# Gated linear attention and a routed mixture of experts: key transposes folded into the score products, single-pass running counts, and a planner that counts instruction pages

## The chip, the cores and the metric

One core of one Trainium2 chip runs the whole program. The metric is the device time of one execution in microseconds; three runs of the kernel before are known, with a median of 393.44 us. One more execution was taken with the hardware profiler, and every row below comes from that one.

## The reference, cut to what matters

The first half is a gated linear attention. For each of 4 batches and 8 heads, 768 steps in order:

```
state = alpha[t][:, None] * state + outer(k[t], v[t])      # 48 x 48 per head
y[t]  = q[t] @ state
```

The second half takes the 3,072 rows of y (384 wide, the heads side by side). For every token it computes logits against 8 experts and one local gate, picks an expert (the argmax, or the expert of the token before it where the gate is at least one half), and computes

```
out[t] = p[e] * (relu(x[t] @ w1[e]) @ w2[e])               # w1: 384 x 1024, w2: 1024 x 384
```

where p is the softmax probability of the chosen expert. Everything is float32.

## The kernel before, in words

**Blocks.** The attention runs in 24 blocks (`NB`) of 128 steps: block i is batch i mod 4 (`G` = 4), part i // 4 of the sequence. So blocks 0 to 3 start the four sequences, from an empty state, and blocks 20 to 23 end them. A block has two chunks c of 64 steps and four head pairs hp; the two heads of a pair, `par` 0 and 1, lie on partitions 64 to 111 and 0 to 47.

**A block's work.** `load` and `load_v` (lines 454 to 479) bring alpha (tile `xa`), keys and queries (`xkq`) and values (`vt`) through SP's queue. `mid` (485) has ACT put ones between the chunks. `scans` (489) has DVE run two reverse running products of alpha over it (`sf`), a reciprocal, and one forward running product (`A`); POOL then multiplies the keys by `sf` and the queries by `A`. `carry` (510) has POOL scale the state that the block takes over. On TensorE: `kt` (522), four transposes of the scaled keys, which ACT copies to the tile `kk`; `pm` (534), 16 score products k^T q, of which ACT copies one half and POOL masks it, while DVE masks the other half (tile `pq`); `um` (572), 8 products of `kk` with the values, which DVE adds to the state (`st`); `ym` (592), 16 products of `pq` with the values (`pv`) and 16 of the queries with the states (`ys`), into one pair of PSUM banks; then ACT copies the result to `XR`, SP stores it in DRAM, and `xt` (637) transposes it for the routing. A float32 product is two matmul instructions, each with a weight load: 16 products show as 32 matmuls.

**Routing.** After every fourth block `route` (662) computes logits, argmax, the gated choice, and each token's place in its expert's list. For the places it adds running counts (lines 731 to 737): the count so far, a triangle times the one-hot choices, and four products with a tile of ones, all float32.

**Experts.** The most popular expert's first 256 tokens are the job "0a" (gathered once 16 blocks are routed), the rest of it "0b", the other experts follow as r1 to r7. Weights and activations are split into a high and a low float32r part; each product is three matmuls. Gathers and stores by token run on POOL's queue.

**What sets the order.** The class `Plan` (76) holds every piece of work as a task: engine, estimated cost, priority, the names it reads and writes, the PSUM banks it needs. `order` (116) simulates the five queues with these costs and takes, on each engine, the open task of the lowest priority number; what it puts out is the program order of each engine, fixed before the run. Where TensorE would be idle for over 0.6 us, it puts products of a zero tile `dz` there ("fill"). `load_` (293) holds a load back until no more than 900 KB (`FLIGHT`) of earlier loads are under way. In `order` nothing stands for the fetching of TensorE's instructions from memory. Nearly all instructions are issued through one helper, so that their line in the profile is 269; they are told apart by the tiles.

Of the kernel before, what the change touches and what calls it, by code (L numbers as in the profile page):

```python
# [19 lines left out]
DM = H * D  # L20
# [4 lines left out]
C = 64  # L25
# [13 lines left out]
HALF = True  # L39
# [18 lines left out]
WS = 9  # L58
NX = dict(a=4, k=6, q=6)
# [11 lines left out]
class Task:  # L71
    __slots__ = ("eng", "cost", "fn", "prio", "deps", "succ", "left", "ready", "alloc", "free", "land", "port", "n", "end",
                 "moe", "start", "ap", "pre", "slack")


class Plan:
# [3 lines left out]
    FILL = 0.112  # L80

# [7 lines left out]
    def add(self, eng, cost, fn, prio, reads=(), writes=(), alloc=None, free=(), land=0.0, port=False, moe=False, after=None, slack=0.0, at=0.0):  # L89
# [3 lines left out]
        t.slack = self.slack + slack  # L93
        deps = set()
# [21 lines left out]
    def order(self, fill_until, fill_from):  # L116
# [6 lines left out]
        held, moe_held = {}, 0  # L123
# [7 lines left out]
        hold = []  # L131
# [19 lines left out]
        while done < len(self.tasks):  # L151
# [33 lines left out]
            if kind is not True:  # L185
                if e == "PE" and fill_from <= now[e] and at > now[e] and now[e] < fill_until(self):
                    n = int((at - now[e] - 0.35) / self.FILL) if at - now[e] > 0.6 else 0
                    b = [x for x, f in free.items() if f <= now[e]]
                    if n > 0 and b:
                        b = min(b, key=lambda x: free[x])  # L190
                        out.append((now[e], len(out), ("fill", b, n)))
                        filled += n * self.FILL
                now[e] = max(at, now[e] + 1e-6)
                continue
# [24 lines left out]
            end = at + t.cost  # L219
            now[e] = end  # L220
# [12 lines left out]
            for nm in t.free:  # L233
                got, m = held.pop(nm)
                for x in got:
                    free[x] = end + 0.06
                if m:
                    moe_held -= len(got)
# [18 lines left out]
def gla_moe(ctx, tc, akq, vw, vn, wg, w1, w2, cst, tok, out):  # L257
# [76 lines left out]
    one = cp.tile([128, 128], F32, name="one")  # L334
    trif = cp.tile([128, 128], F32, name="trif")
# [36 lines left out]
    Xs = dict(a=many(ap, NX["a"], [R, SW + 1], "xa"), kq=many(ap, NX["k"], [128, 2 * BW], "xkq"))  # L372
# [3 lines left out]
    KKs = many(ap, 2, [128, HP, R], "kk")  # L376
# [14 lines left out]
    def setup():  # L391
        add("DVE", 0.3, lambda: v_.memset(zz, 0.0), -9, writes=["zz"])
        add("DVE", 0.2, lambda: v_.tensor_copy(dz, zz[:, 0:256]), -9, reads=["zz"], writes=["dz"])
        add("DVE", 0.3, lambda: v_.memset(Zs, 0.0), -9, writes=["Z"])
        add("DVE", 0.1, lambda: v_.memset(P[0:R, 0, 129:HW:130], 1.0), -9, writes=["Z"])
        for j in range(NV):
            add("POOL", 0.4, lambda j=j: g_.memset(Vs[j][64:128, 0, :], 0.0), -5 + j, writes=[("vz", j)])
        for j in range(G):
            add("POOL", 0.25, lambda j=j: g_.memset(S3s[j][:, 0], 0.0), -4 + j, writes=[("S0", j)])
            add("POOL", 0.35, lambda j=j: g_.memset(S3s[j][96:128, 1:], 0.0), -3.9 + j, writes=[("S1", j), ("S2", j)])  # L400
        add("ACT", 0.4, lambda: s_.dma_start(cs, cst), -3.995, writes=["cs"], land=1.0)
        add("DVE", 0.1, lambda: v_.tensor_copy(DESC, cc("desc")), 2.0, reads=["cs"], writes=["desc"])
        add("ACT", 0.4, lambda: s_.dma_start(tk, tok), -2.5, writes=["tk"], land=0.5)
        add("ACT", 0.5, lambda: s_.dma_start(wgs, wg[:, :, 0:32]), -0.5, writes=["wgs"], land=0.5)
        add("ACT", 0.5, lambda: s_.dma_start(xd[0:1], zz[0:1, :]), 2, reads=["zz"], writes=["xd0"], land=0.1)
        add("POOL", 0.3, lambda: g_.memset(one, 1.0), 2.1, writes=["one"])
        for j in range(2):
            add("POOL", 0.15, lambda j=j: g_.memset(EXs[j][:, :, 8:], 1e-9), 2.2, writes=[("exx", j)])

        def f():  # L410
            g_.tensor_copy(PL[:, 1].rearrange("p (g b) -> p g b", b=G), tk[:, 0:2 * NB:2].rearrange("p (b g) -> p g b", b=G))
            g_.tensor_copy(PL[:, 2], tk[:, 1:2 * NB:2])
            g_.tensor_scalar(PL[:, 1], PL[:, 1], float(-SENT), None, ALU.add)
        add("POOL", 0.7, f, 2.55, reads=["tk"], writes=["plc"])
        kb0 = [e * RS - 1 + e / 16.0 - (16384.0 if e in EARLY else 0.0) for e in range(E)]
        for e in range(E):
            def consts(e=e):
                g_.memset(c0[:, e:e + 1], float(e * RS - 1))
# [3 lines left out]
            add("POOL", 0.4, consts, 2.3, writes=["cst"])  # L422
        add("POOL", 0.6, lambda: (g_.tensor_copy(trif, cc("tri")), g_.memset(trif[0:64, 64:128], 1.0),
                                  g_.memset(trif[64:128, 0:64], 0.0)), 2.4, reads=["cs"], writes=["trif"])
        add("POOL", 0.1, lambda: g_.memset(fill, 0.0), 2.9, writes=["fill"])
        add("PE", 0.3, lambda: t_.matmul(ps("io")[:, 0:128], lhsT=one, rhs=trif, start=True, stop=True), 2.6,
            reads=["one", "trif"], writes=["io"], alloc=("io", 1))
        add("DVE", 0.2, lambda: v_.tensor_scalar(io, ps("io")[:, 0:128], -1.0, None, ALU.add), 2.7, reads=["io"], writes=["iota"],
            free=["io"])

        def f():
            for x in range(NS):
                g_.tensor_scalar(ih[:, x], c0, float(1 + 128 * x), None, ALU.add)
        add("POOL", 0.7, f, 2.8, reads=["cst"], writes=["ih"])

    marks = {}
    OHs = many(rp_, 2, [128, E, G], "oh")
# [11 lines left out]
    def tile_of(c, i):  # L449
        if c == "a":  # L450
            return Xs[c][i % NX[c]]
        return Xs["kq"][i % NX[c]][:, 0:BW] if c == "k" else Xs["kq"][i % NX[c]][:, BW:]

    def load(c, i):
        at = i % G * NBB + i // G

        def go(o, r, w, cost, land, prio, reads, writes):
            add("SP", cost, lambda: load_(i, o, akq[r, at, w]), i - 4 + prio, reads=reads, writes=writes, land=land,
                at=FIRST * max(i - 1, 0) if i < NX[c] else 0.0)
        if c == "a":  # L460
            X, w = Xs["a"][i % NX["a"]], slice(2 * BW, 2 * BW + SW + 1)
            if i < NX["a"]:
                go(X[0:R], slice(0, R), w, 0.4, 0.85, 0, [], kx("a", i))
# [8 lines left out]
        else:  # L472
            for n, r in enumerate((slice(0, D), slice(C, C + D))):
                go(X[r], r, slice(0, 2 * BW), 0.36, 0.56, 0.01 + n * 0.002, [], [(x, i % NX["k"], n) for x in "kq"])

    def load_v(i):
        at, V = i % G * NBB + i // G, Vs[i % NV]
        add("SP", 0.4, lambda: load_(i, V[:, 1, :], vn[:, at * DM:(at + 1) * DM]), i - 1.9, writes=[("v1", i % NV)],
            land=0.55, at=FIRST * i if i < NV else 0.0)
# [42 lines left out]
    def kt(i):  # L522
        k, _ = kq(i)
        kk, nm = KKs[i % 2], f"kp{i}"

        def f():
            kp = ps(nm)[:, 0:HP * R].rearrange("p (h r) -> p h r", h=HP)
            for hp in range(HP):
                t_.transpose(kp[:, hp, :], k[0:R, hp, :], ident[0:R, 0:R])
        add("PE", 0.5, f, i, reads=kx("k", i) + ["cs"], writes=[nm], alloc=(nm, 1))  # L530
        add("ACT", 0.52, lambda: s_.copy(kk.rearrange("p h r -> p (h r)"), ps(nm)[:, 0:HP * R]), i + 0.02, reads=[nm],
            writes=[("kk", i % 2)], free=[nm])

    def pm(i):
        k, q = kq(i)
        pq, nm = PQs[i % 2], f"pe{i}"

        def f():
            pe = ps(nm, 2)
            for hp in range(HP):  # L540
                for (par, c) in ((0, 0), (1, 1), (0, 1), (1, 0)):
                    w = slice(c * C, (c + 1) * C)
                    r = slice(0, C) if par else slice(C, 128)
                    t_.matmul(pe[c * C:(c + 1) * C, par, hp * C:(hp + 1) * C], lhsT=k[r, hp, w], rhs=q[r, hp, w],
                              start=True, stop=True)

        def m():
            v_.tensor_tensor(pq, ps(nm, 2)[:, :, 0:HP * C].rearrange("p e (h t) -> p e h t", h=HP),
                             cc("tri")[:, 0:C].unsqueeze(1).unsqueeze(1).broadcast_to([128, 2, HP, C]), ALU.mult)
        add("PE", 0.65, f, i + 0.1, reads=kx("k", i) + kx("q", i), writes=[nm], alloc=(nm, 2))  # L550
# [4 lines left out]
        def pv(x):  # L555
            return ps(nm, 2)[:, x, 0:HP * C].rearrange("p (h t) -> p h t", h=HP)
        if i >= NB - 2 or MASK(i):
            marks[i] = add("DVE", 0.67, m, i + 0.15, reads=[nm, "cs"], writes=[("pq", i % 2, 0), ("pq", i % 2, 1)], free=[nm])
            return
        if HALF:  # L560
            add("ACT", 0.32, lambda: s_.copy(pq[:, 1], pv(1)), i + 0.14, reads=[nm], writes=[("pq", i % 2, 1)])
            add("POOL", 0.63, lambda: g_.tensor_tensor(pq[:, 1], pq[:, 1], tri(1), ALU.mult), i + 0.15, reads=["cs"],
                writes=[("pq", i % 2, 1)], port=True)
            marks[i] = add("DVE", 0.36, lambda: v_.tensor_tensor(pq[:, 0], pv(0), tri(1), ALU.mult), i + 0.15, reads=[nm, "cs"],
                           writes=[("pq", i % 2, 0)], free=[nm])
            return
        add("ACT", 0.58, lambda: s_.copy(pq, ps(nm, 2)[:, :, 0:HP * C].rearrange("p e (h t) -> p e h t", h=HP)), i + 0.14,
            reads=[nm], writes=[("pq", i % 2, 0), ("pq", i % 2, 1)], free=[nm])
        marks[i] = add("POOL", 1.2, lambda: g_.tensor_tensor(pq, pq, tri(2), ALU.mult), i + 0.15, reads=["cs"],
                       writes=[("pq", i % 2, 0), ("pq", i % 2, 1)], port=True)  # L570
# [823 lines left out]
```

## Time and profile before

| | us |
|---|---|
| median of three runs | 393.44 (391.44 to 393.61) |
| profiled execution, its own time | 390.28 |
| its span, first to last instruction | 388.4 |
| TensorE busy | 359.2 (92%) |
| VectorE (DVE) busy | 227.9 (59%) |
| ScalarE (ACT) busy | 183.0 (47%) |
| GpSimd (POOL) busy | 228.2 (59%) |

The time lies 1.9 us over the span. The span falls into a lead-in (0 to 10.7 us, no TensorE), the attention with its routing (to about 136 us, where the first expert product stands), and the experts. The shares of busy time are means over these; the attention is to be read by itself. A busy TensorE is not one at its peak: the ends of matmuls are modelled, and short products overlap.

### The profile page before, as it was taken

How to read it: one execution, taken by the hardware profiler on the slowest of the kernel's cores; microseconds unless marked ns; L12 is line 12 of the kernel's file. 1: busy time of each engine (PE TensorE's matmuls, PEld its weight loads, DVE VectorE, ACT ScalarE, POOL GpSimd, SP SyncE). 2: the span in 40 equal slices, each digit the busy share in tenths (PEclk: the TensorE clock that was granted, in tenths of full speed). 3: DMA queues.
4: the chain of work that ended last, by engine and by line, in shares of the span. 5: the costliest groups of instructions: out<-in, count | busy, mean ns of one | idle time of the engine just before them, and what ended most of it. 6: DMA issues, size and time to landing. Idle time of an engine off the chain costs nothing. (4 is left out here: it accounts for less than half of the span.)

```text
span 388.4 us, 11793 instructions
## 1 busy us (share of the span) xinstructions
PE 359.2 (92%) x4563; PEld 331.1 (85%) x4563; DVE 227.9 (59%) x545; ACT 183.0 (47%) x514; POOL 228.2 (59%) x329
## 2 busy tenths in 40 slices
PE   0897998988989899999999999999999999999993
PEld 0775787867878799998899999989999999999993
DVE  6796797889887877656434453542551552534320
ACT  2355755865675554374523552560561572542300
POOL 8897686889886523888782465456354354422002
PEclk9998999998999999999999999999999999999999
DMA  7899879869864261756744354553542542321001
GB/s 205 236 238 260 223 186 263 220 198 263 219 197 125 85 222 52 233 160 190 242 117 133 109 154 129 165 160 119 189 138 76 190 135 71 124 83 37 21 8 44
DMA packets 26156, 60.37 MB, mean 155 GB/s; under 512 B 4751, under 2 KB 11116, under 8 KB 26098
## 3 DMA queue, kind: packets, MB, share of 16 engines
q1 hardware_dynamic: 21888, 49.38, 44.0%
q0 software_dynamic: 3520, 9.91, 8.0%
q8 instruction: 37, 0.61, 0.7%
q10 hardware_dynamic: 690, 0.31, 0.3%
q14 instruction: 21, 0.17, 0.1%
HBM read 50.14 MB, written 9.91 MB: 155 GB/s over the span
## 5 line engine op out<-in xcount | busy, mean ns | idle before, releaser
L269 PE MATMUL P<-w2h,hb_mp 128*128 128x384 f32 (+3 forms) x432 | 116.3, 340 | 0.0
L269 POOL TENSOR_TENSOR w1l<-raw,w1h 128x256 fp32r<-128x256 f32 x96 | 70.0, 748 | 45.1 <-ACT w1h L269 33.3
L269 PEld LDWEIGHTS P<-w2h,hb_mp 128*128 128x128 f32 (+3 forms) x432 | 78.0, 185 | 2.0
L269 PE MATMUL P<-w2l,hb_mp 128*128 128x384 f32 (+4 forms) x232 | 78.3, 337 | 0.0
L269 DVE SCALAR_TENSOR_TENSOR hb_mp<-P,hb_mp 128x64 fp32r<-128x64 f32 (+6 forms) x104 | 41.3, 424 | 54.7 <-ACT hb_mp L269 54.3
L269 POOL DMA_INDIRECT out<-yo_mp,LI x27 | 27.4, 1014 | 72.8 <-DVE yo_mp L269 62.6
L269 ACT CAST w2h<-raw 128x384 fp32r<-128x384 f32 x64 | 32.2, 513 | 58.5 <-PE P L269 58.1
L269 PE MATMUL P<-xh_mp,w1h 128*128 128x448 f32 (+5 forms) x168 | 59.5, 354 | 0.0
L269 PE MATMUL P<-xh_mp,w1l 128*128 128x448 f32 (+5 forms) x168 | 59.3, 353 | 0.0
L269 PE MATMUL P<-xl_mp,w1h 128*128 128x448 f32 (+5 forms) x168 | 59.3, 353 | 0.0
L269 ACT ACTIVATE hb_mp<-P 128x448 fp32r<-128x448 f32 (+7 forms) x72 | 34.8, 484 | 52.0 <-PE P L269 47.2
L269 DVE TENSOR_SCALAR yo_mp<-P,LW 128x384 f32<-128x384 f32 (+3 forms) x23 | 14.0, 609 | 59.6 <-PE P L269 59.6
L269 PEld LDWEIGHTS P<-w2l,hb_mp 128*128 128x128 f32 (+4 forms) x232 | 41.4, 178 | 0.4
L269 ACT CAST w1h<-raw 128x256 fp32r<-128x256 f32 x96 | 36.7, 412 | 3.0 <-PE P L269 2.3
L269 DVE TENSOR_TENSOR w2l<-raw,w2h 128x384 fp32r<-128x384 f32 x64 | 35.8, 588 | 3.4 <-ACT w2h L269 3.3
L269 PEld LDWEIGHTS P<-xh_mp,w1l 128*128 128x128 f32 x168 | 31.5, 188 | 1.9
L269 PEld LDWEIGHTS P<-xl_mp,w1h 128*128 128x128 f32 x168 | 31.5, 188 | 1.9
L269 PEld LDWEIGHTS P<-xh_mp,w1h 128*128 128x128 f32 x168 | 31.5, 188 | 1.9
L269 DVE TENSOR_TENSOR_SCAN sf<-xa,P 112x260 f32<-112x260 f32 x48 | 31.3, 677 | 3.0 <-PE P L269 1.5
L269 POOL TENSOR_TENSOR xkq<-xkq,sf 112x512 f32<-112x512 f32 x24 | 28.4, 1182 | 7.2 <-DVE sf L269 5.3
L269 DVE TENSOR_TENSOR_SCAN A<-xa,P 112x520 f32<-112x520 f32 x24 | 29.6, 1233 | 4.0 <-PE P L269 2.2
L269 POOL TENSOR_TENSOR xkq<-xkq,A 112x512 f32<-112x512 f32 x24 | 28.4, 1183 | 3.7 <-DVE A L269 2.7
(159 smaller groups left out, 595.3 us busy)
## 6 DMA issues: line engine op xcount, KB each, us to landing
raw<-w SPq DMA_DIRECT2D x24, 512.0 KB, 3.8
raw<-w SPq DMA_DIRECT2D x32, 384.0 KB, 4.3
xkq<-akq SPq DMA_DIRECT2D x36, 192.0 KB, 4.6
vt<-vn SPq DMA_DIRECT2D x24, 192.0 KB, 4.1
xd<-XR SPq DMA_DIRECT2D x24, 192.0 KB, 4.5
xa<-akq SPq DMA_DIRECT2D x40, 97.7 KB, 4.2
xkq<-akq SPq DMA_DIRECT2D x12, 224.0 KB, 3.6
xa<-akq SPq DMA_DIRECT2D x4, 227.9 KB, 3.8
```

The lines of the kernel that those rows point to most:

```text
L269: r = f(*a, **k)
```

## The change

1. **Keys.** `kt` is gone. `pm` gives each of its 16 products a moving operand of 128 columns instead of 64: 64 columns of queries and a 64-column identity that is kept at the end of the tile `xkq`. The second half of each result is the transposed keys. ACT copies these to `kk` from the same PSUM banks, after its copy for `pq`.
2. **States.** In blocks 0 to 3, `ys` leaves out the products with the empty state of chunk 0, and the state is copied instead of added. In blocks 20 to 23, `um` computes only the first chunk's part (48 columns instead of 96).
3. **Running counts.** `one`, `trif` and the one-hot tile become float32r, with the layout block by expert; five of the six products become one matmul each.
4. **Planner.** It counts TensorE's instructions (`ins`), has a page of 256 of them, and stalls TensorE at a page's end until a fetch of 5.3, 4.6 or 3.6 us (by the time) that began when the page was entered is through. PSUM banks come free after the last task that uses them.
5. **Lead-in.** 28 zero products (`WARM`) run on TensorE ahead of the first block. The first activation-table load is forced early on ACT by an exponential of one element. Clears of tiles are spread over DVE, POOL and ACT; small constants leave POOL's early queue; the constants' load is cut in two and waits for the table; `mid` runs on DVE for blocks 0 and 1; the first loads come in another order, and those of the first two blocks are not held back by `FLIGHT`.

```diff
-HALF = True
+WARM = 28
+    PAGE, LEAD = 256, 63
+    def fetch(at):
+        return 5.3 if at < 45 else 4.6 if at < 110 else 3.6
...
+            if e == "PE":
+                c = count
+                count += t.ins
+                while count > edge:
+                    over = max(at, at + t.cost * (edge - c) / t.ins + end - at - t.cost)
+                    if over < there:
+                        self.stalled += there - over
+                        end += there - over
+                        over = there
+                    there = over + self.fetch(over)
+                    edge += self.PAGE
...
+        if n < 2:
+            return r
         flight.append((r.ins.name, o.shape[0] * o.free_size() * 4 / 1024))
...
-    one = cp.tile([128, 128], F32, name="one")
-    trif = cp.tile([128, 128], F32, name="trif")
+    one = cp.tile([128, 128], F32R, name="one")
+    trif = cp.tile([128, 128], F32R, name="trif")
-    Xs = dict(a=many(ap, NX["a"], [R, SW + 1], "xa"), kq=many(ap, NX["k"], [128, 2 * BW], "xkq"))
+    Xs = dict(a=many(ap, NX["a"], [R, SW + 1], "xa"), kq=many(ap, NX["k"], [128, 2 * BW + C], "xkq"))
-    KKs = many(ap, 2, [128, HP, R], "kk")
+    KKs = many(ap, 2, [128, 2, HP, C], "kk")
...
+        def warm():
+            for _ in range(WARM):
+                t_.matmul(ps("warm")[:, 0:240], lhsT=dz[:, 0:128], rhs=dz[:, 0:240], start=True, stop=True)
+        add("PE", WARM * 0.155, warm, -9, ins=2 * WARM, reads=["dz"], writes=["warm"], alloc=("warm", 1), free=["warm"])
-        add("ACT", 0.4, lambda: s_.dma_start(cs, cst), -3.995, writes=["cs"], land=1.0)
+        add("ACT", 0.4, lambda: s_.dma_start(cs[:, 0:256], cst[:, 0:256]), -8.9, reads=["table"], writes=["cs"], land=0.55)
+        add("ACT", 0.4, lambda: s_.dma_start(cs[:, 256:], cst[:, 256:]), -2.6, writes=["cs2"], land=0.45, at=6.0)
...
+        if i < 2:
+            add("DVE", 0.1, lambda: v_.memset(a[:, C + 1:SW:2 * (C + 1)], 1.0), i - 1.6, writes=kx("a", i))
+            return
...
-    def kt(i):
...
-                t_.transpose(kp[:, hp, :], k[0:R, hp, :], ident[0:R, 0:R])
-        add("PE", 0.5, f, i, reads=kx("k", i) + ["cs"], writes=[nm], alloc=(nm, 1))
-        add("ACT", 0.52, lambda: s_.copy(kk.rearrange("p h r -> p (h r)"), ps(nm)[:, 0:HP * R]), i + 0.02, reads=[nm],
-            writes=[("kk", i % 2)], free=[nm])
...
-                    t_.matmul(pe[c * C:(c + 1) * C, par, hp * C:(hp + 1) * C], lhsT=k[r, hp, w], rhs=q[r, hp, w],
-                              start=True, stop=True)
+                    x = X[r, at:at + C]
+                    t_.matmul(pe[c * C:(c + 1) * C, par, hp * 128:(hp + 1) * 128], lhsT=k[r, hp, c * C:(c + 1) * C],
+                              rhs=bass.AP(x.tensor, x.offset, [x.ap[0], (2 * BW - at, 2), (1, C)]), start=True, stop=True)
-        add("PE", 0.65, f, i + 0.1, reads=kx("k", i) + kx("q", i), writes=[nm], alloc=(nm, 2))
+        add("PE", 0.9, f, i + 0.1, ins=64, reads=kx("k", i) + kx("q", i) + [("xi", i % NX["k"])], writes=[nm], alloc=(nm, 2))
+        kc = lambda: add("ACT", 0.58, lambda: s_.copy(kk, part(1)), i + 0.145, reads=[nm], writes=[("kk", i % 2)], free=[nm])
...
+                    if i < G and not c:
+                        continue
...
-            t_.matmul(o, lhsT=ident, rhs=c_in.unsqueeze(2).broadcast_to([128, E, n + 1]), start=True, stop=False)
-            t_.matmul(o[:, :, 0:n], lhsT=trif, rhs=oh, start=False, stop=False)
+            t_.matmul(o, lhsT=ident, rhs=c_in.unsqueeze(1).broadcast_to([128, n + 1, E]), start=True, stop=False)
+            t_.matmul(o[:, 0:E * n], lhsT=trif, rhs=ot, start=False, stop=False)
             for x in range(1, n + 1):
-                t_.matmul(o[:, :, x:], lhsT=one, rhs=oh[:, :, 0:n + 1 - x], start=False, stop=(x == n))
+                t_.matmul(o[:, E * x:], lhsT=one, rhs=ot[:, 0:E * (n + 1 - x)], start=False, stop=(x == n))
...
+    add("ACT", 1.4, lambda: s_.activation(mark, one_r[0:1, 0:1], AF.Exp), -9, reads=["oner"], writes=["table"])
+    pads = ["DVE", "POOL", "ACT", "POOL", "ACT", "ACT"]
...
+    for j in range(NX["k"]):
+        for h in range(2):
+            r = slice(h * C, (h + 1) * C)
+            add("ACT", 0.2, lambda j=j, r=r: s_.copy(Xs["kq"][j][r, 2 * BW:], ident[r, r]), -6.5 + j, reads=["cs"],
+                writes=[("xi", j)])
...
-        kt(i)
```

## Rows read from the trace of the kernel before

**Rows 1.** Stretches: us; busy PE, PEld, DVE, ACT, POOL (instructions); clock, DMA, GB/s.
```profile
10.00:130.00 120.00, 106.92 (x2925) 90.66 (x2926) 99.61 (x234) 72.76 (x241) 97.74 (x143) 0.97 0.78 212
133.00:383.00 250.00, 249.27 (x1550) 237.61 (x1549) 119.65 (x287) 106.02 (x264) 119.88 (x144) 1.00 0.41 129
```
**Rows 2.** What TensorE waited for: us in total, times, longest.
```profile
PE P L269 <- POOL xkq L269: 10.7, 1, 10.7
PE P L269 <- issue: 7.6, 8, 2.2
```
**Rows 3.** TensorE in order of time, around 30 us: start, us, what.
```profile
28.50 0.80 PE L269 MATMUL P<-vt,pq 64*64 64x48 f32 x18
31.48 0.44 PE L269 MATMUL P<-vt,pq 64*64 64x48 f32 x14 [2.19 <-issue]
```
**Rows 4.** Stretches between such waits, the wait itself, and what follows it.
```profile
29.30:31.40 2.10, 0.00 (x0) 0.00 (x0) 1.96 (x5) 1.33 (x4) 2.04 (x3) 1.00 1.00 259
31.48:37.30 5.82, 5.16 (x127) 4.48 (x126) 2.80 (x7) 3.73 (x12) 3.65 (x5) 0.71 0.99 266
37.30:42.62 5.32, 4.48 (x127) 3.55 (x127) 4.40 (x8) 3.08 (x10) 5.32 (x7) 1.00 0.88 206
56.66:66.81 10.15, 8.72 (x253) 7.52 (x253) 8.33 (x20) 6.54 (x21) 7.50 (x10) 1.00 0.89 251
```
**Rows 5.** Instruction queue: packets, MB, share; whole span, 10 to 130 us, 136 to 384 us.
```profile
q8 instruction: 37, 0.61, 0.7%
...
q8 instruction: 23, 0.38, 1.5%
...
q8 instruction: 13, 0.21, 0.4%
```
**Rows 6.** The lead-in, in order of time; the median landing of the first alpha loads.
```profile
0.72 0.88 SPq L269 DMA_DIRECT2D xa<-akq  x2
5.70 1.28 ACT L269 ACT_TABLE_LOAD   x1 [5.70 <-DVE P L269]
7.22 1.28 DVE L269 TENSOR_TENSOR_SCAN sf<-xa,P 112x260 f32<-112x260 f32 x2 [1.45 <-ACT xa L269]
9.47 1.17 POOL L269 TENSOR_TENSOR xkq<-xkq,sf 112x512 f32<-112x512 f32 x1
...
xa<-akq SPq DMA_DIRECT2D x4, 227.9 KB, 3.8
```
**Rows 7.** TensorE in order of time: transposes and the next start; scores at 13.81 and 15.91.
```profile
18.77 0.60 PE L269 MATMUL P<-cs,xkq 112*128 112x112 f32 x4
19.21 0.49 PE L269 MATMUL P<-cs,XR 128*128 128x128 f32 x3
...
13.81 1.13 PE L269 MATMUL P<-xkq 64*64 64x64 f32 x32
...
15.91 0.69 PE L269 MATMUL P<-xkq 64*64 64x64 f32 x32
```
**Rows 8.** The same: products with states, with values, and a running count with its end.
```profile
17.35 0.68 PE L269 MATMUL P<-st,xkq 64*64 64x48 f32 x32 [0.29 <-ACT mark L269]
17.96 0.88 PE L269 MATMUL P<-vt,kk 128*48 128x96 f32 x16
...
130.56 0.39 PE L269 MATMUL P<-oh,trif 128*128 128x32 f32 x2
130.79 1.04 PE L269 MATMUL P<-oh,one 128*128 128x32 f32 x8
131.76 0.45 PE L269 MATMUL P<-st,xkq 64*64 64x48 f32 x16
```
**Rows 9.** ACT's two copies for a block, then all engines from 20 to 30 us.
```profile
15.03 0.37 ACT L269 COPY pq<-P 128x256 f32<-128x256 f32 x1 [2.66 <-PE P L269]
15.67 0.53 ACT L269 COPY kk<-P 128x448 f32<-128x448 f32 x1 [0.27 <-PE P L269]
...
20.00:30.00 10.00, 9.00 (x283) 7.34 (x275) 9.69 (x19) 4.51 (x15) 9.70 (x20) 1.00 0.94 246
```

More of the change, by code (lines that the diff above doesn't have):

```diff
@@ L87, in __init__, with add @@
         self.slack = 0.0
-    def add(self, eng, cost, fn, prio, reads=(), writes=(), alloc=None, free=(), land=0.0, port=False, moe=False, after=None, slack=0.0, at=0.0):
+    def add(self, eng, cost, fn, prio, reads=(), writes=(), alloc=None, free=(), land=0.0, port=False, moe=False, after=None, slack=0.0, at=0.0, ins=6):
         t = Task()
@@ L93, in add @@
         t.slack = self.slack + slack
+        t.ins = ins
+        t.uses = {k for k in (*reads, *writes) if isinstance(k, str)}
         deps = set()
@@ L130, in order @@
         filled = 0.0
-        hold = []
+        count, edge, there = self.LEAD, self.PAGE, 0.0
+        self.stalled = 0.0
+        users = {}
+        for t in self.tasks:
+            for k in t.uses:
+                users[k] = users.get(k, 0) + 1
         def fits(t, at):
@@ L232, in order @@
             t.end = fin
[L233 to L238, printed above, removed]
+            for nm in t.uses:
+                users[nm] -= 1
+                last[nm] = max(last.get(nm, 0.0), end)
+                if users[nm] == 0 and nm in held:
+                    got, m = held.pop(nm)
+                    for x in got:
+                        free[x] = last[nm] + 0.06
+                    if m:
+                        moe_held -= len(got)
             self.ap_left -= t.ap
@@ new lines, in warm @@
+        def warm():
+            for _ in range(WARM):
+                t_.matmul(ps("warm")[:, 0:240], lhsT=dz[:, 0:128], rhs=dz[:, 0:240], start=True, stop=True)
+        add("PE", WARM * 0.155, warm, -9, ins=2 * WARM, reads=["dz"], writes=["warm"], alloc=("warm", 1), free=["warm"])
+        for j in range(NV):
+            if j < 2:
+                add("POOL", 0.4, lambda j=j: g_.memset(Vs[j][64:128, 0, :], 0.0), -5 + j, writes=[("vz", j)])
+            else:
+                add("ACT", 0.5, lambda j=j: s_.copy(Vs[j][64:128, 0, :], zz[64:128, :]), -6 + j / 10, reads=["zz"],
+                    writes=[("vz", j)])
@@ L405, in setup @@
         add("ACT", 0.5, lambda: s_.dma_start(xd[0:1], zz[0:1, :]), 2, reads=["zz"], writes=["xd0"], land=0.1)
-        add("POOL", 0.3, lambda: g_.memset(one, 1.0), 2.1, writes=["one"])
+        add("DVE", 0.1, lambda: v_.tensor_copy(DESC, cc("desc")), 2.0, reads=["cs2"], writes=["desc"])
+        add("ACT", 0.25, lambda: s_.activation(one, zz[:, 0:128], AF.Copy, bias=1.0), 2.95, reads=["zz"], writes=["one"])
         for j in range(2):
-            add("POOL", 0.15, lambda j=j: g_.memset(EXs[j][:, :, 8:], 1e-9), 2.2, writes=[("exx", j)])
+            add("POOL", 0.15, lambda j=j: g_.memset(EXs[j][:, :, 8:], 1e-9), 3.0, writes=[("exx", j)])
@@ L415, in setup @@
+            s_.copy(PL[:, 2], tk[:, 1:2 * NB:2])
+        add("ACT", 0.4, f, 3.3, reads=["tk"], writes=["plc"])
         kb0 = [e * RS - 1 + e / 16.0 - (16384.0 if e in EARLY else 0.0) for e in range(E)]
@@ L421, in consts @@
                 g_.memset(lens[:, e:e + 1], float(LEN[e]))
[L422 to L426, printed above, removed]
+            add("POOL", 0.08, lambda e=e: g_.memset(c0[:, e:e + 1], float(e * RS - 1)), 3.2, writes=["cst0"])
+            add("POOL", 0.24, consts, 9.5 + e / 2, writes=["cst"], at=30.0 + 3 * e)
+        add("POOL", 0.6, lambda: (g_.tensor_copy(trif, cc("tri")), g_.tensor_copy(trif[0:64, 64:128], one.bitcast(F32)[0:64, 0:64]),
+                                  g_.tensor_copy(trif[64:128, 0:64], zz[64:128, 0:64])), 3.05, reads=["cs", "one", "zz"],
+            writes=["trif"])
+        add("POOL", 0.1, lambda: g_.memset(fill, 0.0), 4.9, writes=["fill"])
+        add("PE", 0.3, lambda: t_.matmul(ps("io")[:, 0:128], lhsT=one, rhs=trif, start=True, stop=True), 3.1, ins=4,
             reads=["one", "trif"], writes=["io"], alloc=("io", 1))
[L428 removed]
+        add("DVE", 0.2, lambda: v_.tensor_scalar(io, ps("io")[:, 0:128], -1.0, None, ALU.add), 3.2, reads=["io"], writes=["iota"],
             free=["io"])
@@ L458, in go @@
             add("SP", cost, lambda: load_(i, o, akq[r, at, w]), i - 4 + prio, reads=reads, writes=writes, land=land,
-                at=FIRST * max(i - 1, 0) if i < NX[c] else 0.0)
+                at=(0.0, 1.2)[i] if c == "a" and i < 2 else FIRST * max(i - 1, 0) if i < NX[c] else 0.0)
         if c == "a":
@@ L555, in pv @@
         def pv(x):
-            return ps(nm, 2)[:, x, 0:HP * C].rearrange("p (h t) -> p h t", h=HP)
+            return part(0)[:, x]
         if i >= NB - 2 or MASK(i):
-            marks[i] = add("DVE", 0.67, m, i + 0.15, reads=[nm, "cs"], writes=[("pq", i % 2, 0), ("pq", i % 2, 1)], free=[nm])
+            marks[i] = add("DVE", 0.67, m, i + 0.15, reads=[nm, "cs"], writes=[("pq", i % 2, 0), ("pq", i % 2, 1)])
+            kc()
             return
[L560 to L570, printed above, removed]
+        add("ACT", 0.32, lambda: s_.copy(pq[:, 1], pv(1)), i + 0.14, reads=[nm], writes=[("pq", i % 2, 1)])
+        add("POOL", 0.63, lambda: g_.tensor_tensor(pq[:, 1], pq[:, 1], tri(1), ALU.mult), i + 0.15, reads=["cs"],
+            writes=[("pq", i % 2, 1)], port=True)
+        marks[i] = add("DVE", 0.36, lambda: v_.tensor_tensor(pq[:, 0], pv(0), tri(1), ALU.mult), i + 0.15, reads=[nm, "cs"],
+                       writes=[("pq", i % 2, 0)])
+        kc()
     def um(i):
@@ L602, in pv @@
                     t_.matmul(yw[half(par, c), par, hp * D:(hp + 1) * D], lhsT=pq[r, par, hp, :], rhs=vt[r, h * D:(h + 1) * D],
-                              start=(hp == 0), stop=False, skip_group_check=True)
+                              start=(hp == 0), stop=(i < G and not c and hp == HP - 1), skip_group_check=True)
         def ys():
@@ L1130, in gla_moe @@
     one_r = ap.tile([R, HP], F32, name="one_r")
-    add("DVE", 0.1, lambda: v_.memset(one_r, 1.0), -9, writes=["oner"])
-    for n, (c, j) in enumerate((c, j) for j in range(max(NX.values())) for c in "kq" if j < NX[c]):
-        add("DVE" if n < 6 else "POOL", 0.55, lambda c=c, j=j, n=n: (v_ if n < 6 else g_).memset(tile_of(c, j)[96:128], 0.0),
-            -9.9 + n * 0.05 if n < 6 else -6.5 + n / 2, writes=[("xz", c, j)])
+    add("DVE", 0.1, lambda: v_.memset(one_r, 1.0), -9.95, writes=["oner"])
+    add("DVE", 0.36, lambda: v_.memset(zz, 0.0), -9.5, writes=["zz"])
+    add("DVE", 0.45, lambda: v_.tensor_copy(dz, zz[:, 0:256]), -8.95, reads=["zz"], writes=["dz"])
+    add("ACT", 1.4, lambda: s_.activation(mark, one_r[0:1, 0:1], AF.Exp), -9, reads=["oner"], writes=["table"])
+    pads = ["DVE", "POOL", "ACT", "POOL", "ACT", "ACT"]
+    for j in range(NX["k"]):
+        p = Xs["kq"][j][96:128, 0:2 * BW]
+        if pads[j] == "ACT":
+            add("ACT", 1.05, lambda p=p: s_.copy(p, zz[96:128, 0:1].broadcast_to([32, 2 * BW])), -8 + j, reads=["zz"],
+                writes=[("xz", c, j) for c in "kq"])
+        else:
+            for n, c in enumerate("kq"):
+                w = ("DVE", "POOL")[n] if j == 0 else pads[j]
+                e = dict(DVE=v_, POOL=g_)[w]
+                add(w, 0.53, lambda p=p, e=e, n=n: e.memset(p[:, n * BW:(n + 1) * BW], 0.0), -9.9 + j + n / 10,
+                    writes=[("xz", c, j)])
     for i in range(max(NX.values())):
@@ L1142, in gla_moe @@
             setup()
+    for j in range(NX["k"]):
+        for h in range(2):
+            r = slice(h * C, (h + 1) * C)
+            add("ACT", 0.2, lambda j=j, r=r: s_.copy(Xs["kq"][j][r, 2 * BW:], ident[r, r]), -6.5 + j, reads=["cs"],
+                writes=[("xi", j)])
     mp_box = []
```

109 lines of the change are left out of this document (52 added, 57 removed).

## The prediction

> **What bounds the kernel now.** First the busy times by stretch [rows 1]. From 133 us to the end TensorE works 249.27 of 250 us: the experts are TensorE's, the change touches nothing in them, and they start when the attention lets them. So the question is how much earlier TensorE gets through the attention. There, from 10 to 130 us, it is busy 106.9 of 120 us, DVE 99.6, POOL 97.7: three engines in fixed orders, none free by much, TensorE nearest to full.
>
> Second, TensorE's waits [rows 2]: 10.7 us for the first scaled keys, then mostly "issue", 7.6 us in 8 waits, up to 2.2 us, where no other engine is waited for. Third, such a wait in order of time [rows 3]: a run of 32 equal products breaks after 18 and goes on 2.19 us later, with no operand new. Fourth, the instructions between these waits [rows 4]: from 31.48 to 37.30 us 127 matmuls and 126 weight loads, then 127 and 127, then (two steps) 253 and 253. With a few semaphore waits each step is 256. Fifth, the instruction queue [rows 5]: 37 packets of 16 KB in the whole span, 23 of them in these 120 us, 13 in the 248 us of the experts. So TensorE's program arrives in pages of about 256 instructions, and in the attention, where 32 products take 0.69 us [rows 7], a page is used up about as fast as the next arrives: 120 / 23 = 5.2 us a page on average, and 5.32, 5.82 and 5.08 us in steps that ended in a wait [rows 4], with the data transfers busy 88 to 99%. During the wait itself they are at 100% [rows 4].
>
> **The change, part by part,** against the profiled execution's 390.28 us.
>
> *Lead-in.* DVE's first scan stands at 7.22 us, behind ACT's fill-in of ones, which stands behind a table load from 5.70 to 6.98 us [rows 6]. The first alpha tile is issued at 0.72 us and lands after about 3.8 us [rows 6], at 4.5. With DVE writing the ones itself (0.1 us by the planner's cost), the scan starts near 4.6: 2.6 us earlier. POOL's first multiply, at 9.47 us behind its clears, can follow the two scans at 4.6 + 1.28 = 5.9, or when the clears left to it are through (five pads, two value and four state clears, about 0.5 us each by the planner's costs: 0.7 + 5.5 = 6.2). That is 3.3 us earlier, and DVE's 2.6 decides. Both queues are full from 20 to 30 us, 9.7 of 10 [rows 9], so a shift of both is kept. **-2.6 us**; bounds 0 (alpha lands no sooner than ACT was ready, 7 us) and -4.5 (POOL's constants, which leave its queue too). The identity copies, the other pads and the table go to ACT, which first works at 5.70 us [rows 6]. The constants, now issued behind the table, about 0.9 + 1.3 us, land near 6 if they take 3.8 like the alpha tiles; the identity copies then have until the first scores at 6.2 + 2 x 1.17 = 8.5, so I cost them at 0. If the constants land later, the scores wait for them, and the gain goes towards the bound of 0.
>
> *Warm-up.* Early scores took 1.13 us at 13.81 and 0.69 at 15.91 [rows 7]: the first ran at half clock. I take 0, since DVE and POOL pace this stage; -2 if TensorE does. Its cost: 56 instructions.
>
> *Keys.* Four transposes go: the next group starts 19.21 - 18.77 = 0.44 us later than they do [rows 7]. The scores get twice the columns. No row has 128 columns at full clock; 64 at half clock take the same array time, 1.13 against 0.69 us [rows 7], so 0.44 us is added. Bounds: 0 to +0.44 (0 if issuing, not columns, paces the 32 products). I take the upper end: in array time the swap gives **nothing**. In instructions it removes 8 in each of 24 blocks, 192.
>
> *States and counts.* `ys` halved in four blocks: 4 x 0.34 = 1.4 us [rows 8], 128 instructions. `um` at half width in four: towards the 0.68 of 48-column products from 0.88 [rows 8], 4 x 0.2 = 0.8. Counts: triangle and ones take 131.76 - 130.56 = 1.2 us for ten matmuls [rows 8], half of them go, six times: 3.6 us, 60 instructions. Work removed: 5.8 us.
>
> *Pages.* 192 + 128 + 60 - 56 = 324 instructions less, 1.27 pages, at 5.2 us **6.6 us if every page is paced by its fetch**. If none is, the work removed counts: 5.8. By rows, 8 of 23 pages end in a wait, so 0.35 x 6.6 + 0.65 x 5.8 = **-6.1 us**. The two ends lie close, so the weight hardly matters, as long as TensorE is the bound.
>
> [...]
>
> *Planner.* The order of all five queues is made anew, with stalls in it. It removes no fetch; it can put work where a stall would hit less. Bounds: -7.6 (all issue waits [rows 2] hidden), and above 0 what a new wait costs (second rival). I take 0.
>
> *What else waits.* `kk` now comes out after the scores and after ACT's copy for `pq`: 0.37 + 0.53 us [rows 9] stand between scores and state product, where before the scores lay between transposes and state product. TensorE has products of other blocks to put there (`pv`, `ys`, each 0.6 us), so I cost it at 0; uncovered it is 0.9 us a block. The two score banks are held for it longer, but the transposes' bank is gone. DVE's and POOL's work in a block is the same.
>
> Sum: -2.6 - 6.1 = -8.7, so 381.6 for a run like the profiled one. The median of the runs stands 393.44 - 390.28 = 3.2 us higher: **384.7**.
>
> **Rivals.**
> - *DVE and POOL hold it.* TensorE gets lighter, but both are full from 20 to 30 us [rows 9] and above 80% after [rows 1]; half the gain is lost in waits for them: 393.44 - 4.4 = 389. Against: both have some 20 us of idle in 120. It falls on either side of 1%.
> - *The stalls go altogether.* A lighter page and an order that knows of them hide most of the 7.6 us, and the half clock after the longest (0.71 from 31.48 to 37.30 [rows 4]) goes too: 8 us more, 376.5. Against: pages that took 5.3 us at full transfer load still do.
> - *Nothing at the start.* If alpha lands late, 384.7 + 2.6 = 387.3.
> - *Slower: late keys.* TensorE, in order, meets the state product before `kk` is there. Price up to 0.9 us a block; it decides from 8.7 / 24 = 0.36 us. At 0.6 us: 14.4 - 8.7 = +5.7, 399. For: ACT already waits often and stands behind its `mark` and result copies. Against: a planner that knows the dependency.
>
> **The numbers.** Forecast 0.42, DVE and POOL 0.26, stalls gone 0.12, nothing at the start 0.08, late keys 0.12. A measurement here tells about 1% (389.5 to 397.4) from no change. Faster: 0.42 + 0.12 + 0.08 + 0.11 of the second case = 0.73; within 1%: the other 0.15; slower: 0.12. The range from 377 to 392 leaves out late keys above it and half of the stalls gone below: 0.18.
>
> **What would show it.** Lead-in: first scan near 4.6 us, POOL's first multiply near 6.2, scores by 9. Pages: 22 or fewer instruction packets before the experts start, and "issue" waits again 256 instructions apart; if such waits stand elsewhere, my reading of them is wrong. Keys: scores of about 1.1 us at full clock, no transposes; late keys would show as TensorE waiting for ACT `kk`. DVE and POOL: their idle in the attention falls below a tenth while TensorE waits for `sf`, `A` or `xkq`. The first expert product, now at about 136 us, should stand near 127; if it does and the end does not follow, the experts were held by something I did not see.

## The result and the profile after

The median went from 393.02 us (four runs) to **387.01 us** (four runs, 385.95 to 388.11), a ratio of 0.9854 (95% interval 0.9807 to 0.9900). In two later groups with twelve runs each of the changed kernel, each on one chip beside runs of the kernel before, the ratio was 0.9949 (0.9906 to 0.9991) and 0.9927 (0.9891 to 0.9962). So the gain is real and between 0.5 and 1.5%. Some executions run a per cent or more longer at a lower granted clock (of the kernel before in the last group, one took 388.36 us at 0.989 and one 403.60 at 0.959); the medians here include them and the ratios leave them out, so differences below go by the ratios. The experiments of a group are compared with the runs of that group. The profiled execution after took 387.89 us (span 386.1), 2.4 less than the one before.

The same stretches after, as in [rows 1]:

```profile
10.00:130.00 120.00, 105.47 (x2838) 88.83 (x2838) 101.23 (x241) 77.16 (x254) 95.60 (x138) 1.00 0.79 214
133.00:383.00 250.00, 246.68 (x1533) 235.57 (x1532) 114.63 (x276) 104.59 (x260) 119.52 (x142) 1.00 0.41 129
```

TensorE is as busy as before, DVE a little busier. TensorE's waits from 10 us on, as in [rows 2]:

```profile
PE P L297 <- issue: 3.5, 4, 1.9
PE P L297 <- DVE A L297: 2.5, 3, 1.0
PE P L297 <- DVE kr L297: 1.7, 2, 1.4
PE P L297 <- POOL st L297: 1.5, 1, 1.5
```

The "issue" waits halved, 7.6 to 3.5 us; waits for other engines took their place. Three of the four stand on the edge of a page of 256 instructions, as before: from the first to the second TensorE ran 380 matmuls and 380 weight loads, and from the second to the fourth 379 and 381, each time 760 or three pages less a few. The third, 0.42 us, stands between edges.

```profile
61.93:77.07 15.14, 13.89 (x380) 11.49 (x380) 14.06 (x37) 11.03 (x40) 14.24 (x18) 1.00 0.84 228
77.07:89.15 12.08, 10.20 (x287) 8.08 (x288) 10.22 (x24) 8.62 (x27) 10.12 (x15) 1.00 0.90 240
89.15:94.57 5.42, 3.47 (x92) 2.83 (x93) 4.01 (x9) 3.58 (x13) 4.85 (x6) 1.00 0.96 264
```

The instruction queue from 10 to 130 us, as in [rows 5], brought 22 packets instead of 23:

```profile
q8 instruction: 22, 0.36, 1.3%
```

The lead-in in order of time, as in [rows 6], and on to the first output (lines picked from several engines):

```profile
4.14 1.28 DVE L297 TENSOR_TENSOR_SCAN sf<-xa,P 112x260 f32<-112x260 f32 x2
6.83 1.18 POOL L297 TENSOR_TENSOR xkq<-xkq,sf 112x512 f32<-112x512 f32 x1
7.96 1.20 POOL L297 TENSOR_TENSOR xkq<-xkq,A 112x512 f32<-112x512 f32 x1
2.84 9.64 PE L297 MATMUL P<-dz 128*128 128x240 f32 x59 [2.84 <-DVE dz L297]
8.26 0.63 ACTq L297 DMA_DIRECT2D wgs<-wg  x1
8.93 3.07 ACT L297 COPY xkq<-cs 64x64 f32<-64x64 f32 x12 [1.64 <-DMA xkq<-akq]
12.41 1.10 PE L297 MATMUL P<-xkq 64*64 64x128 f32 x32
13.57 0.42 DVE L297 TENSOR_TENSOR pq<-P,cs 128x256 f32<-128x256 f32 x1 [3.12 <-PE P L297]
14.03 0.59 ACT L297 COPY kk<-P 128x512 f32<-128x512 f32 x1
15.21 0.88 PE L297 MATMUL P<-vt,kk 128*48 128x96 f32 x16
18.66 0.97 ACT L297 COPY XR<-P 128x192 f32<-128x192 f32 x3
```

The first scan is 3.1 us earlier and POOL's first multiply 2.6. But the first block's output stood at 18.08 us before, as this line of ACT in the trace before shows:

```profile
18.08 0.97 ACT L269 COPY XR<-P 128x192 f32<-128x192 f32 x3 [0.42 <-PE P L269]
```

It is now at 18.66 (17.47 in the other profile of the changed kernel that is used below). In between TensorE ran 59 zero products until about 12.4, 28 of the warm-up and 31 that the planner put behind them, though the queries were ready at 9.16; DVE meanwhile waited 3.1 us for the scores; and ACT ran all twelve identity copies in a row. In the whole run there are 105 zero products, before 12.

The first expert product came at 131.9 us instead of 136.0, 4.1 us earlier.

### The profile page after: what moved, and what is told of

Same layout as the page of the kernel before. It is cut to its first block, busy times and chain, and to the rows that moved or that the text cites. A ratio compares the mean times of both kernels' runs of the same rounds, so it can differ in the third digit from the quotient of the medians.

```text
span 386.1 us, 11571 instructions
## 1 busy us (share of the span) xinstructions
PE 362.3 (94%) x4465; PEld 334.1 (87%) x4465; DVE 225.8 (58%) x542; ACT 191.6 (50%) x537; POOL 225.6 (58%) x314
## 5 line engine op out<-in xcount | busy, mean ns | idle before, releaser
L297 ACT CAST w2h<-raw 128x384 fp32r<-128x384 f32 x64 | 32.5, 513 | 58.5 <-PE P L297 58.0
L297 PE MATMUL P<-xkq 64*64 64x128 f32 x768 | 26.8, 275 | 3.9 <-issue 2.4
```

Of the source, the lines that this page charges most:

```text
L297: r = f(*a, **k)
```

## Experiments

**Group one: zero products and the planner.** First the changed kernel itself.

> The changed kernel itself, unchanged, so that the others of this group can be compared with it on one chip. Expected: 387.0 us as before, 1.5% below the kernel before.

Measured: 389.36 us (12 runs; before 393.09), ratio 0.9949 (0.9906 to 0.9991). A smaller gain than in the first comparison. Its profile from 10 to 130 us, to compare with the next:

```profile
10.00:130.00 120.00, 107.10 (x2840) 90.10 (x2842) 101.04 (x241) 77.32 (x256) 95.38 (x138) 0.97 0.79 214
```

```diff
         if isinstance(t, tuple):
-            for _ in range(t[2]):
-                t_.matmul(P[:, t[1], 0:240], lhsT=dz[:, 0:128], rhs=dz[:, 0:240], start=True, stop=True)
             continue
```

> The changed kernel without the zero products that the planner puts into TensorE's gaps (77 of them); the 28 of the warm-up stay, and the order of everything else stays as it is. Theory (the zero products gave part of the lead-in back): the first scores could start at about 9.4 us, where their queries and identity are ready, but wait behind zero products until 12.4; without them they start near 9.4, and 154 instructions, 0.6 of a page, are gone as well: 383.5 to 385. Rival (DVE and POOL pace the lead-in and the blocks after it): the scores start earlier, the blocks after them do not, 386.5 to 387.5. Second rival (the zero products keep the clock up): half clock returns in the first 20 us, 388 or more.

Measured: 389.43 us, ratio 0.9937 (0.9895 to 0.9978): no difference. The stretch from 10 to 130 us, and TensorE's and then ACT's start:

```profile
10.00:130.00 120.00, 98.61 (x2702) 81.98 (x2694) 100.34 (x239) 75.56 (x250) 95.59 (x138) 0.97 0.80 213
...
9.21 1.10 PE L297 MATMUL P<-xkq 64*64 64x128 f32 x32
12.79 1.55 PE L297 MATMUL P<-vt,kk 128*48 128x96 f32 x16 [2.22 <-ACT kk L297]
```
```profile
8.41 3.05 ACT L297 COPY xkq<-cs 64x64 f32<-64x64 f32 x12 [1.13 <-DMA vt<-vn]
12.16 0.58 ACT L297 COPY kk<-P 128x512 f32<-128x512 f32 x1
17.64 0.97 ACT L297 COPY XR<-P 128x192 f32<-128x192 f32 x3
```

The scores did move to 9.21 us, as the theory said, but the transposed keys come from ACT only behind the twelve identity copies, the state product waits 2.2 us for them and then takes 1.55 us instead of 0.88, and the output is at 17.64. The granted clock in that stretch was 0.50:

```profile
12.80:14.40 1.60, 1.60 (x20) 1.38 (x24) 0.72 (x2) 0.44 (x2) 0.26 (x1) 0.50 1.08 264
```

So the second rival's half clock came too, and what it cost is in the 389.43. The main reading is the first row: without zero products TensorE has 98.6 us of work in 120, 8.5 us less than in the profile above, DVE 100.3; the program ends no sooner. That fits the first rival. It is not proof that TensorE's time does not count: the planner had put the zero products where it saw TensorE idle, so taking them out need not free anything. For that, work has to be added (group three).

```diff
-            for _ in range(WARM):
+            for _ in range(1):
```

> As the run without fills, and the warm-up is one zero product instead of 28. Theory of the zero products: their 56 instructions go too, the first scores and state products run at half clock (0.4 and 0.7 us more each), which the idle of TensorE there can hide: 383 to 385, equal to the run without fills within 1 us. Rival (the warm-up earns its place): 1 to 2.5 us slower than the run without fills.

Measured: 391.16 us, ratio 0.9995 (0.9964 to 1.0027), 1.7 us above the run without fills by the medians and 2.3 by the ratios. That is the rival's direction: the warm-up products seem to earn their place. The intervals overlap a little, so this is likely and its size open.

```diff
     def fetch(at):
-        return 5.3 if at < 45 else 4.6 if at < 110 else 3.6
+        return 0.0
```

> The changed kernel, planned with a fetch time of 0, so that no page ever stalls the planned TensorE; all the work is the same, its order and the number of zero products are planned anew. Theory of the forecast (the planner's counting is worth nothing by itself, the gain is in the instructions and the lead-in): 386 to 388. Rival (knowing the stalls is what turned 7.6 us of issue waits into 3.5): issue waits return to 6 us or more, and the time to 389.5 to 391.

Measured: 389.17 us, ratio 0.9934 (0.9900 to 0.9969): no difference from the changed kernel. Its waits on fetches did return:

```profile
PE P L297 <- issue: 6.3, 10, 1.4
PE P L297 <- POOL pq L297: 1.3, 1, 1.3
```

So the planner's counting moves waits from one name to another, 6.3 us of "issue" against 2.1 in the profile of the changed kernel in this group, and the time stays, within some 2 us. In this run, in those of group two that undo parts, and in the last of group three, the planner makes the order anew, with other numbers of zero products (63 to 119 instead of 105). Each difference therefore also holds what the new order changes; no run separates the two.

**Group two: parts undone.** The measure again:

> The changed kernel itself again, as the measure for the others of this group on the same chip. Expected: 386 to 390 us, 0.5 to 1.5% below the kernel before.

Measured: 389.21 us (12 runs; before 390.93), ratio 0.9927 (0.9891 to 0.9962).

```diff
+        add("PE", 0.5, f, i, ins=8, reads=kx("k", i) + ["cs"], writes=[nm], alloc=(nm, 1))
...
-        add("PE", 0.9, f, i + 0.1, ins=64, ...
+        add("PE", 0.65, f, i + 0.1, ins=64, ...
```

The first line is `kt`, the four transposes; the other two are the scores, back to 64 columns.

> The changed kernel with the keys transposed as in the kernel before: four transposes a block with their own copy, scores with 64 columns, no identity copies; the planner counts 8 instructions for the transposes. Theory of the forecast (instructions decide): 192 instructions more, 0.75 page, 1.5 to 4 us slower than the changed kernel. Rival (TensorE's instructions are no longer what decides between 10 and 130 us): within 1 us of the changed kernel.

Measured: 390.16 us, ratio 0.9958 (0.9930 to 0.9987): 0.3%, 1.2 us, above the changed kernel, inside the uncertainty. Neither theory is decided: by the two intervals the difference lies between -0.6 and 3 us.

```diff
-                    if i < G and not c:
-                        continue
...
-    one = cp.tile([128, 128], F32R, name="one")
+    one = cp.tile([128, 128], F32, name="one")
...
-        n = 2 if i + G < NB else 1
+        n = 2
```

> The changed kernel with the products with the empty states, the full-width state products of the last blocks and the float32 running counts back in. Theory of the forecast: 5.8 us of work and 188 instructions come back, 3 to 6 us slower than the changed kernel. Rival (TensorE has the time for them): within 1.5 us.

Measured: 390.80 us, ratio 0.9981 (0.9950 to 1.0011): 0.54%, 2.1 us, above the changed kernel, about a third of the 5.8 us of work put back (0.3 to 3.9 by the intervals). Between the two theories. Part of the 5.8 was never there: the halved products with the states (x16, changed kernel) take as long as the full ones (x32, 17.35 to 17.96 us in [rows 8]), by the next start 0.60 us instead of 0.61:

```profile
17.92 0.67 PE L297 MATMUL P<-st,xkq 64*64 64x48 f32 x16 [0.35 <-ACT mark L297]
18.52 0.72 PE L297 MATMUL P<-dz 128*128 128x240 f32 x4
```

> The changed kernel with the old keys, the full states, the float32 counts and a planner whose fetches take no time: what is left of the change is the lead-in (and banks that come free with the last task that uses them). Theory of the forecast: 2.6 us below the kernel before. Rival (the lead-in's gain is lost again before the first block's output, which stands at 18.7 us before and 18.1 to 19.3 after): within 1 us of the kernel before.

(All of the above edits together, with the fetch time of 0.) Measured: 390.67 us, ratio 1.0001 (0.9964 to 1.0038). The lead-in alone gains nothing in the end, as the rival said, but not for its reason. In this run the lead is not lost ahead of the first output: that stands at 15.12 us, 3.0 earlier than in the kernel before, and the last one at 135.88, 3.3 earlier (first two lines this run, third line before):

```profile
15.12 0.32 ACT L297 COPY XR<-P 128x192 f32<-128x192 f32 x1 [0.81 <-PE P L297]
135.88 0.97 ACT L297 COPY XR<-P 128x192 f32<-128x192 f32 x3
139.21 0.97 ACT L269 COPY XR<-P 128x192 f32<-128x192 f32 x3 [1.00 <-PE P L269]
```

It is lost among the experts. TensorE, ahead of time, waits 1.75 us for the gather of the tokens (`xg_mp`) of a later job, and soon after the granted clock falls, 0.83 on the mean from 160 to 170 us:

```profile
158.62 0.55 PE L297 MATMUL P<-cs,xg_mp 128*128 128x128 f32 x3 [1.75 <-DMA xg_mp<-xd,LI]
160.00:170.00 10.00, 10.00 (x76) 9.92 (x74) 3.96 (x18) 6.60 (x21) 6.68 (x9) 0.83 0.34 99
```

The wait and 0.17 of 10 us make some 3.4 us, an estimate of what was lost there; the kernel before has neither (clock 1.00, TensorE busy 20.0 of 20 us from 150 to 170). The first product of that job (`xh_mp`) is at 176.6 us in both profiles. The parts, 1.2 + 2.1 + 0, add up to 3.3 us, and the whole change gained 0.73% of 390.93, 2.9 us, in this group.

**Group three: work added, and the lead-in mended.**

```diff
-        add("DVE", 1.24, lambda: v_.tensor_tensor_scan(A, a[:, 0:SW], ZB, 1.0, ALU.mult, ALU.add), i - 1.1,
+        add("DVE", 1.24, lambda: (v_.tensor_tensor_scan(A, a[:, 0:SW], ZB, 1.0, ALU.mult, ALU.add), v_.memset(scr, 0.0)), i - 1.1,
```

> The changed kernel with one clear of a spare tile (128 x 512) behind each block's forward scan on DVE, about 0.5 us in each of 24 blocks, 12 us in all; nothing reads it, and the order is unchanged. Theory DVE (it paces the attention): 8 to 12 us slower than the changed kernel. Theory TensorE or pages: 0 to 3 us slower.

Measured: 395.93 us (before 392.60), ratio 1.0056 (1.0011 to 1.0100).

```diff
+            for _ in range(16):
+                t_.matmul(uw[0:32, 400:402], lhsT=dz[0:32, 0:32], rhs=dz[0:32, 0:2], start=True, stop=True)
```

> The changed kernel with 16 products of 2 columns behind each block's state products: 32 instructions a block, 768 in all, 3 pages, about 0.35 us of TensorE a block, 8 us in all. Theory pages: 10 to 16 us slower than the changed kernel. Theory TensorE's time: 5 to 8 us, as much as the next run. Theory DVE: 0 to 3 us.

Measured: 394.62 us, ratio 1.0065 (1.0030 to 1.0100).

```diff
+            for _ in range(3):
+                t_.matmul(uw[0:112, 384:512], lhsT=dz[:, 0:112], rhs=dz[:, 0:128], start=True, stop=True)
```

> The changed kernel with 3 float32r products of 128 columns behind each block's state products: 6 instructions a block, 144 in all, and 0.3 us of TensorE a block, 7 us in all. Theory pages: 1 to 3 us slower than the changed kernel, far less than the run with 32 instructions. Theory TensorE's time: 5 to 7 us. Theory DVE: 0 to 3 us.

Measured: 393.24 us, ratio 1.0054 (1.0018 to 1.0090).

TensorE and the instruction queue from 10 to 130 us, with 32 instructions a block and then with 6:

```profile
10.00:130.00 120.00, 114.18 (x3059) 98.59 (x3057) 95.93 (x227) 75.08 (x245) 95.62 (x138) 0.99 0.78 214
...
q8 instruction: 24, 0.39, 1.4%
```
```profile
10.00:130.00 120.00, 110.66 (x2777) 93.55 (x2775) 99.52 (x229) 74.98 (x245) 95.81 (x138) 0.99 0.79 212
...
q8 instruction: 22, 0.36, 1.4%
```

The 16 short products took 0.59 us a block in the trace, the 3 long ones about 0.44, so 14 and 10.5 us were added on TensorE, and 11.6 on DVE (24 x 0.485). None of this passed whole. The changed kernel itself was not run in this group; against 0.9938, the mean of its two groups of twelve on other chips, the three are 4.6, 5.0 and 4.6 us slower, each uncertain by about 2 us: 0.40 of DVE's added time, 0.35 and 0.44 of TensorE's. And 624 instructions more, 2.4 pages, made 0.0011 or 0.4 us between the last two (1.4 by the medians, uncertain by some 2 us); at the forecast's 5.2 us a page it would have been 12.7. Theory pages falls. Of the two theories of one pacing engine, neither fits all three runs: DVE's is missed by each of them, TensorE's asked for 0 to 3 us in the first run and gets its 5 us in the others only because more was added than planned. With the planner's zero products left in TensorE's gaps, added time of either engine passes at about 0.4, by the uncertainty 0.2 to 0.6.

TensorE's part of this is not TensorE's time alone. The added products stand in the state product's task, and DVE's `st`, which takes over its result, waits for them too (with 32 instructions a block, then the changed kernel):

```profile
DVE st L297 <- PE P L297: 5.5, 7, 1.2
DVE st L297 <- PE P L297: 1.1, 2, 0.6
```

```diff
-... s_.copy(Xs["kq"][j][r, 2 * BW:], ident[r, r]), -6.5 + j, reads=["cs"],
+... s_.copy(Xs["kq"][j][r, 2 * BW:], ident[r, r]), (-6.5 if j == 0 else j - 1.2), reads=["cs"],
...
-    order = pl_.order(lambda p: 0.0 if hasattr(J1.first, "start") else 1e9, 5.0)
+    order = pl_.order(lambda p: 0.0 if hasattr(J1.first, "start") else 1e9, 14.0)
```

> The changed kernel with two edits to the lead-in: the identity copies for blocks 1 to 5 get a late priority on ACT (only block 0's stand early), and the planner puts no zero products before 14 us of its time (the 28 of the warm-up stay). Theory (ACT's twelve identity copies and the zero products hold the first blocks): the first state product moves from 13.8 to 15.2 us to 11 or 12, the first block's output from 18 to 19 us to about 16, and the end by 1 to 2 us against the changed kernel, 1.5 to 2% below the kernel before. Rival (the blocks after it are paced elsewhere): first output earlier, the end within 1 us of the changed kernel.

Measured: 386.79 us (six runs), ratio 0.9873 (0.9822 to 0.9923). TensorE, then ACT, in order of time:

```profile
9.64 1.10 PE L297 MATMUL P<-xkq 64*64 64x128 f32 x32 [1.47 <-POOL trif L297]
12.04 0.88 PE L297 MATMUL P<-vt,kk 128*48 128x96 f32 x16 [1.04 <-ACT kk L297]
```
```profile
11.41 0.58 ACT L297 COPY kk<-P 128x512 f32<-128x512 f32 x1
14.60 0.97 ACT L297 COPY XR<-P 128x192 f32<-128x192 f32 x3 [0.79 <-PE P L297]
```

With the planner's zero products ahead of the first scores gone and ACT's copies spread (seven of the twelve still run ahead of `kk`) the first output stands at 14.60 us, 4.1 earlier than in the changed kernel (2.9 than in its other profile) and 3.5 earlier than before: that the two held the first output is shown. That the first output sets the end is not: the fifth output, at 40.03 us, is later than the changed kernel's at 37.02, and the last, at 132.27, is 4.9 earlier than its 137.12, while this execution's span, 384.1 us, is 2.0 shorter.

```profile
40.03 0.99 ACT L297 COPY XR<-P 128x192 f32<-128x192 f32 x3
132.27 0.97 ACT L297 COPY XR<-P 128x192 f32<-128x192 f32 x3 [0.23 <-PE P L297]
```

This version is faster than the kernel before. Against the changed kernel (0.9854, 0.9949, 0.9927) its interval overlaps all three, and they did not run in one group, so that it beats it is likely and not shown.

## Why the forecast came out as it did

The forecast was 384.7 us in a range of 377 to 392; the first comparison gave 387.0, on the side that was forecast, 6.0 us of the 8.7. The later groups make it 2.0 and 2.9 us. So the direction was forecast for reasons that partly held, and that 387.0 came so near is in part luck: the range is 15 us wide, and the parts that were forecast at 8.7 us measured 3.3. The step that is off is the one that the working itself named as its condition: "as long as TensorE is the bound".

- **Bound.** Wrong. That TensorE was "nearest to full" was read as busy time that sets the end. Added time on it passed at 0.35 to 0.44, not at 1. The rival "DVE and POOL hold it", half the gain lost, 389, is nearest to the larger groups in the number, but its sign did not come: DVE was idle for 16% and POOL for 20% of the 120 us, not below a tenth, and TensorE waited 2.5 us for `A` and not at all for `sf` or `xkq`. Nor was it DVE alone: its added time passed at about 0.4 as well.
- **Pages.** The mechanism fits [rows 3 to 5]: waits stand whole pages of 256 instructions apart, and after the change three of four do. The sign "22 or fewer packets before the experts start" was missed by one: 22 from 10 to 130 us, but 23 up to 132 us. The price was wrong: -6.1 us for pages and work together measured 3.3 in undone parts (1.2 for the keys, 2.1 for states and counts). Here waits for other engines took the place of waits on a fetch ("issue" 7.6 us before and 3.5 after, `A` 0.5 and 2.5, POOL's `st` none and 1.5). So the waits on fetches exist, but instructions by themselves earned nothing that the runs can tell: 624 more of them made 0.4 us, uncertain by some 2.
- **States.** The 1.4 us for the halved `ys` were mis-sized: halving the products left their time at 0.54 to 0.60 us against 0.61 to 0.62, together 0.1 to 0.2 us in four blocks. The halved width of `um` (0.60 us to the next start instead of 0.81) and of the counts (0.6 us instead of 1.2) came as forecast.
- **Instructions.** 324 fewer were forecast; matmuls and weight loads fell by 2 x (4563 - 4465) = 196. The warm-up's 28 zero products were in the sum; 65 more that the planner put into gaps, 130 instructions, were not.
- **Lead-in.** Scan at 4.6 us forecast, 4.14 measured; multiply 6.2, 6.83; scores "by 9", 12.41. In the changed kernel the -2.6 us was lost between the queries and the first output; where it was not lost there, it was lost later: the lead-in alone measured 0.0 (within 1.5) with a first output 3.0 us and a last one 3.3 us earlier.
- **Keys.** Scores of 128 columns at full clock: 1.13 us forecast from half clock, 1.10 measured at a granted clock of 1.00. That is 0.41 more than the 0.69 for 64 columns, against 0.44 for the transposes, so the swap is indeed nothing in TensorE's time. Late keys, the slower rival, cost little: TensorE waited for `kk` 0.2 us in all. But in the first blocks zero products stand where it would have waited; without them it waited 3.6 us in 3 waits, 2.2 of them in the first block, far from a wait in each of 24 blocks.
- **Warm-up and planner** were costed at 0. The planner held; for the warm-up the runs lean to 2 us of gain. That the first scores ran at half clock is an estimate from their 1.13 us: the trace has a granted clock of 1.00 there. It fits the times, since 32 such products took 1.13 us at 93.80 us of the same trace too, at a granted clock of 0.50, and 0.66 at 98.90, at 1.00. In the same way the first state product of the kernel before (at 12.32 us, granted clock 1.00) took 1.55 us, as one did at 0.50 in the run without fills; later ones took 0.88.
- **Stalls and clock.** The granted clock from 10 to 130 us was 0.97 before, 1.00 in the first profile after and 0.97 in the next one, which was the faster execution (387.03 against 387.89 us). So the half clock behind a stall, which a rival priced (0.50 from 32.5 to 35.5 us in the kernel before, after the wait of 2.19), is not what made the gain. (That rival's sum is 376.7, not 376.5.)
- **Tail.** The last block's forward scan came at 118.96 us instead of 125.42, 6.5 us ahead, but its output copies only at 137.12 to 138.09 instead of 139.21 to 140.18, 2.1 us ahead. There, from 117 to 137 us, DVE works 16.9 of 20 us and TensorE 18.4 (before 16.8 and 18.6), with routing and low weight parts among the attention; that this is what holds the last block is argued, not shown. The first expert product was to stand near 127 us; it came at 131.9, 4.1 us earlier than before, and the span ended 2.3 us earlier. So of the 8.7 us, 4.1 were there at the experts' start and 2.1 at the last block's output.

**Open:** what carries the 0.4. ACT and POOL were not probed, nor the run of waits from block to block that fixed orders make, nor how much of any difference is the new order. The lead-in-only run shows one place where a lead is lost, the first gathers of the experts, in one execution; whether it is so in the changed kernel was not tested (its profile has no such wait). And why the first comparison gained twice what the later ones did.

## What to carry to other kernels

Where three engines in fixed orders are each 80 to 90% busy, the busiest need not be the bound (here time added on it passed at 0.35 to 0.44): price saved work by adding some and seeing what part of it comes out at the end, before summing terms at full value, and see that nothing else waits for what was added. A stall that is real in the trace is worth only what the next wait behind it leaves: 6.3 us of "issue" waits and 2.1 ended in the same time here, within some 2 us. A gain at the start has to be followed past every in-order queue, filler work included, and not only to the first output: it can reach the end of its stage and be lost in the next, as the 3.3 us of the lead-in-only run were.

## What the runs showed of the hardware that was not expected

Pages can come faster than the 5.2 us read from before: with 32 instructions a block added, 24 packets came in the same 120 us, 5.0 us each, with fewer waits ("issue" 1.6 us). In the run without fills a state product of the first block took 1.55 us, not 0.88, after a wait of 2.2 us, and the granted clock was 0.50 from 12.80 to 14.40 us, after 1.00 from 0 to 10 us: the warm-up's full clock did not outlast that wait. Half the products need not take half the time: 16 matmuls of `ys` took 0.54 to 0.60 us, all 32 took 0.61 to 0.62. The trace lists both as products of 64x64 tiles (`64*64`); why the time stays was not shown.
